# Another first pair of an attention and mixture-of-experts kernel: loads by head, first maxima with 64 rows, value work ahead of the exponentials

## The chip, the cores and the metric

The kernel runs on one core of a Trainium2 chip. The metric is the device time of one execution in microseconds (us), the median of several runs. One execution is recorded by the hardware profiler; its trace gives every row in this document. TensorE is PE, VectorE is DVE, ScalarE is ACT, GpSimd is POOL, and SyncE is SP, which only issues transfers.

## The reference: pooled-query attention, then a mixture of experts

Only the attention matters here. For 8 batches of 8 heads, 1152 positions and 64 dimensions each:

```python
q_pool = q.reshape(B, H, S // factor, factor, D).mean(axis=3)      # 576 queries
scores = scale * np.matmul(q_pool, k.transpose(0, 1, 3, 2))
scores = scores - np.max(scores, axis=-1, keepdims=True)
attn = np.exp(scores)
attn = attn / (np.sum(attn, axis=-1, keepdims=True) + 1e-09)
return np.matmul(attn, v).astype(np.float32)
```

The result (4608 tokens of 512) is routed to one of 8 experts, each of two matrix products.

## The kernel before

**Pairs.** The attention runs over 32 pairs. A pair is the same head of two batches: head one (of the pair) lies on partitions 0 to 63, head two on 64 to 127. `load_kq` and `load_v` bring keys `rawk` (128 x 1152), queries `rawq` (two halves of 576 columns, which are added for the pooling) and values `rawv`. Fetching runs ahead: while one pair's exponentials are made, the next pair is split and placed, and the one after is loaded.

**Exact products from 16-bit parts.** Keys and queries are split into a rounded part (`hi`, `qh`, by ACT) and a rest (`lo`, by POOL, seven subtractions). SP's queue then copies them into `B1` and `B2` of the pair (`place_q`, `place_k`, `place_lo`; tile `B` in the trace), from which each score is two matmuls (`scores`, lines 877 and 878). A row of `B2` holds the negative maximum of every query, in 16 bits (`mr`), so that the matmul subtracts it.

**Maxima.** A rough score from `hi` and the rounded queries `QB` gives the maxima. `QB` is block-diagonal: 9 blocks `u` of 128 queries, 0 to 3 and the lower half of 4 of head one, the rest of head two; what a head doesn't use is zero, cleared by DVE at the start. For pair 0, `first_max` multiplies blocks 0 to 4 with three thirds of the keys in 15 matmuls (`psc` and `pm` are banks of PSUM), and DVE reduces each (line 836); `row` then takes the maximum (`m`), has PE transpose it (line 783) and DVE round it (`mr`), and a transfer on ACT's queue writes it into `B2` (line 793). `maxpass` does blocks 5 to 8 of pair 0, and all of later pairs, between the scores (lines 812, 820).

**Exponentials and values.** A bank of 432 scores is exponentiated by ACT into `Pe` (line 879), four for each of six groups of a pair; the low half of the exponential's bits, `Pl`, is made by ACT (line 860) and DVE (line 862). The values get a common power of two as scale: ACT squares and sums them (`square`, line 720), PE sums over partitions (`power`), DVE makes the scale in five small operations (`scales`). `values` rounds them to `VH` (ACT, two parts) and makes the rest `vl` (POOL for pairs 0 and 1); `shifted` makes `VS`, a copy of `VH` times 2^-16. `pv` multiplies: three matmuls on `VH`, `vl` and `VS`.

**What sets the order.** The order on each engine is the order in which the program is written; an engine waits at an instruction until its inputs are there, with all behind it. Before the loop the first pair is written out by hand. In the loop each step writes some scores, maxima and value products, and tables give the step at which a pair's work is written. For pair 0, `V0` does so for the squares, the scale, `VH`, `VS` and `vl`; `LAG0` is the number of steps between a group of exponentials and its products with the values. The transfers share eight semaphores: each waits for the one eight earlier.

Of the kernel before, what the change touches and what calls it, by code (L numbers as in the profile page):

```python
# [574 lines left out]
def attention(tc, ctx, att, ident, npairs, xpool, on_two, on_split, on_scale, jobs, side, set_pm, started, ahead, hip):  # L575
# [35 lines left out]
    half_q = lambda i: slice(i * 288, (i + 1) * 288)  # L611

    def load_kq(p):
        k, q = (pa.tile([P, S], F32, name="raw" + x) for x in "kq")
        st[p]["k"], st[p]["q"] = k, q
        if p == 0:
            two = lambda x: x.rearrange("p (w n) -> p w n", w=2)
            for x, i in ((q, 0), (k, 0), (k, 1), (q, 1), (k, 2)):
                if x is q:
                    nc.sync.dma_start(out=two(q)[:, :, half_q(i)], in_=two(att[p, :, S:2 * S])[:, :, half_q(i)])  # L620
# [144 lines left out]
    def shifted(p):  # L765

        need(p, "vh0", "vh1")
        made.add((p, "vs"))
        o, v = (flat(x[p % 3])[:, :, 0:D] for x in (VS, VH))
        if p:  # L770
            nc.vector.tensor_single_scalar(o, v, 2.0 ** -16, op=ALU.mult)
        else:
            nc.scalar.activation(o, v, AF.Copy, scale=2.0 ** -16)
# [55 lines left out]
    def first_max(p):  # L829
# [3 lines left out]
        for i, (u, t) in enumerate([(u, t) for us in ((0, 1), (2, 3, 4)) for t in range(3) for u in us]):  # L833
            pt = ps_sc.tile([P, 512], F32, name="psc") if i % 2 else ps_max.tile([P, 512], F32, name="pm")
            nc.tensor.matmul(pt[:, 0:384], QB[p % 2][:, u], s["hi"][:, t * 384:(t + 1) * 384], start=True, stop=True)
            nc.vector.tensor_reduce(mp[:, u, t:t + 1], pt[:, 0:384], op=ALU.max, axis=AX.X)
# [170 lines left out]
    nc.scalar.activation(warm, warm, AF.Exp)
# [11 lines left out]
    for n, i in ((0, 0), (2, 1), (2, 2)):  # L1019
        if i < 2:  # L1020
            both = st[0]["q"].rearrange("p (w n) -> p w n", w=2)
            nc.vector.tensor_tensor(both[:, 0, half_q(i)], both[:, 0, half_q(i)], both[:, 1, half_q(i)], op=ALU.add)
        if i == 0:
            nc.scalar.copy(qb[0:D, half_q(0)], q0[0:D, half_q(0)])
        split_hi(0, i)
        if i == 1:
            nc.scalar.copy(qb[0:D, half_q(1)], q0[0:D, half_q(1)])
# [22 lines left out]
    drain(first)  # L1050
    mp0 = st[0]["mp"]
    for i in range(3):
        nc.gpsimd.memset(VH[i][:, :, :, D:D + 2], 1.0)
        nc.gpsimd.memset(VS[i][:, :, :, D:D + 2], 2.0 ** -16)
    for pe, pl in PT:
        for x in (slice(0, D), slice(D + W3, 2 * D + W3)):
            nc.gpsimd.memset(pe[:, x].bitcast(F32), 0.0)
            nc.gpsimd.memset(pl[:, x], 0.0)
    nc.gpsimd.memset(B2[1][D:D + 1, 0:2 * S], ROW)
# [472 lines left out]
```

## Time and profile before

| | us |
|---|---|
| median of 3 runs | 1150.68 (1149.37 to 1151.63) |
| the profiled execution | 1149.96 |
| its span | 1148.3 |
| busy: PE, DVE, ACT, POOL | 1105.8, 978.9, 914.7, 419.5 |
| first rough score on PE | 5.16 after the start |
| first exponential | 19.24 |
| first product with values | 31.05 |

A row of the timeline has its start and its duration in us, the engine, the line of the kernel, the operation with its output and input, and in brackets how long the engine had been idle and what ended that. A duration includes the latency of the result, so instructions of one engine can overlap. SPq and ACTq are issues of transfers; when the data land is not in the row.

### The profile page before, as it was taken

Reading aid. Unit: us, or ns where it says so; the run is one execution under the profiler, and the core shown is the slowest. Engines: PE = TensorE matmul, PEld = TensorE weight load, DVE = VectorE, ACT = ScalarE, POOL = GpSimd, SP = SyncE. Lnnn points to the kernel's source line nnn. Section 1 sums busy time; section 2 is a strip of 40 time slices with the busy share of each in tenths; the row PEclk is TensorE's granted clock in tenths of the full one; section 3 lists DMA queues with packets and bytes.
Section 4 is the critical chain, followed back from the end, with each engine's and each line's share of the span. In section 5 each row is a group of like instructions: output and inputs, shape, how many; then the busy total and the mean of one; then the engine's idle time right before and its main releaser. Section 6 shows DMA issues by size and latency. Waiting matters only on the chain. (4 is left out here: it accounts for less than half of the span.)

```text
span 1148.3 us, 36571 instructions
## 1 busy us (share of the span) xinstructions
PE 1105.8 (96%) x14963; PEld 813.4 (71%) x14963; DVE 978.9 (85%) x1961; ACT 914.7 (80%) x1463; POOL 419.5 (37%) x408
## 2 busy tenths in 40 slices
PE   5999999999999999999999989999999999999995
PEld 2777777777777777777777767866676676766763
DVE  6999999999999999999999999888976667576661
ACT  5999999999999999999999989766556666565561
POOL 6854444454453454434445331233222311211201
PEclk9999999999999999999999999999999999999998
DMA  7767858867758768669768463699989999989970
GB/s 226 195 174 177 192 156 175 191 162 181 190 149 203 172 165 199 156 170 193 171 167 185 129 132 77 222 279 283 283 243 267 316 274 295 278 268 285 252 250 22
DMA packets 175568, 232.65 MB, mean 203 GB/s; under 512 B 92351, under 2 KB 126799, under 8 KB 175392
## 3 DMA queue, kind: packets, MB, share of 16 engines
q1 hardware_dynamic: 169254, 210.45, 70.8%
q0 software_dynamic: 6128, 19.78, 6.4%
q8 instruction: 119, 1.95, 0.7%
q14 instruction: 57, 0.47, 0.2%
q10 hardware_dynamic: 10, 0.00, 0.0%
HBM read 146.11 MB, written 19.18 MB: 144 GB/s over the span
## 5 line engine op out<-in xcount | busy, mean ns | idle before, releaser
L879 ACT ACTIVATE Pe<-psc 128x432 int32<-128x432 f32 x768 | 377.7, 526 | 46.0 <-PE psc L878 36.0
L813 DVE TENSOR_REDUCE mp<-pm 128x1 f32<-128x512 f32 x566 | 373.3, 684 | 16.8 <-PE pm L812 8.9
L936 PE MATMUL xp<-VH,Pe 128*128 128x65 f16 x2880 | 372.6, 193 | 0.0
L938 PE MATMUL xp<-VS,Pl 128*128 128x65 f16 x2880 | 371.9, 193 | 0.4 <-DVE Pl L862 0.4
L937 PE MATMUL xp<-vl,Pe 128*128 128x64 f16 x2880 | 370.7, 192 | 0.0
L937 PEld LDWEIGHTS <-Pe 128*128 128x128 f16 x2880 | 267.6, 98 | 87.6
L878 PE MATMUL psc<-B 65*128 65x432 f16 (+2 forms) x1152 | 305.7, 288 | 2.2 <-DMA B<-mr 2.2
L877 PE MATMUL psc<-B 128*128 128x432 f16 (+2 forms) x1152 | 305.0, 287 | 1.7 <-ACT Pe L879 1.5
L936 PEld LDWEIGHTS <-Pe 128*128 128x128 f16 x2880 | 272.0, 98 | 45.7 <-issue 7.9
L938 PEld LDWEIGHTS <-Pl 128*128 128x128 f16 x2880 | 266.5, 97 | 0.6 <-DVE Pl L862 0.5
L860 ACT ACTIVATE Pl<-Pe 128x1152 f16<-128x1152 uint16 (+1 forms) x190 | 219.3, 1154 | 6.0
L812 PE MATMUL pm<-hi,QB 128*128 128x512 f16 x566 | 215.1, 382 | 8.4 <-DVE mp L813 8.1
L761 POOL TENSOR_SCALAR VH<-rawv,sc 128x512 f16<-128x512 f32 (+1 forms) x60 | 103.4, 1732 | 154.3 <-PE xp L938 73.7
L674 POOL TENSOR_TENSOR lo<-rawk,hi 128x576 f16<-128x576 f32 (+1 forms) x68 | 87.7, 1292 | 196.9 <-ACT hi L658 184.0
L1271 PE MATMUL ph<-xpart,w1h 128*128 128x256 f16 x544 | 148.3, 273 | 0.0
L1273 PE MATMUL ph<-xpart,w1l 128*128 128x256 f16 x544 | 148.3, 273 | 0.0
L1272 PE MATMUL ph<-xpart,w1h 128*128 128x256 f16 x544 | 148.3, 273 | 0.0
L878 PEld LDWEIGHTS <-B 65*128 65x128 f16 x1152 | 113.1, 98 | 26.8 <-issue 3.3
L877 PEld LDWEIGHTS <-B 128*128 128x128 f16 x1152 | 112.8, 98 | 9.7 <-issue 4.5
L1318 PE MATMUL po<-w2l,hh 128*128 128x512 f16 x296 | 112.2, 379 | 0.0
L1319 PE MATMUL po<-w2h,hl 128*128 128x512 f16 x296 | 112.2, 379 | 0.0
L1317 PE MATMUL po<-w2h,hh 128*128 128x512 f16 x296 | 112.2, 379 | 0.0
(260 smaller groups left out, 1775.9 us busy)
## 6 DMA issues: line engine op xcount, KB each, us to landing
w2r<-in_w_dram SPq DMA_DIRECT2D x76, 512.0 KB
w1r<-in_w_dram SPq DMA_DIRECT2D x72, 512.0 KB
rawv<-in_att_dram SPq DMA_DIRECT2D x32, 576.0 KB
B<-hi SPq DMA_DIRECT2D x128, 144.0 KB
rawq<-in_att_dram SPq DMA_DIRECT2D x31, 576.0 KB
rawk<-in_att_dram SPq DMA_DIRECT2D x31, 576.0 KB
B<-qh SPq DMA_DIRECT2D x128, 72.0 KB
B<-lo SPq DMA_DIRECT2D x64, 144.0 KB
```

Source lines behind the costliest of these rows:

```text
L812: nc.tensor.matmul(pm, QB[p % 2][:, u], s["hi"][:, t * 512:(t + 1) * 512], start=True, stop=True)
L813: nc.vector.tensor_reduce(mp[:, u, t:t + 1], pm, op=ALU.max, axis=AX.X)
L860: nc.scalar.activation(low, rest, AF.Copy, scale=LOW)
L877: nc.tensor.matmul(o, b1[:, ks], b1[:, qs], start=True, stop=False, skip_group_check=True)
L878: nc.tensor.matmul(o, b2[:, ks], b2[:, qs], start=False, stop=True, skip_group_check=True)
L879: nc.scalar.activation(Pe[:, D + x0:D + x1], pt, AF.Exp, scale=1.0 / 16)
L936: nc.tensor.matmul(out, Ph[:, qs], vh[:, c, j, 0:D + 1], start=c == 0 and g == 0, stop=False, skip_group_check=True)
L937: nc.tensor.matmul(out[:, 0:D], Ph[:, qs], vl[:, c, j], start=False, stop=False, skip_group_check=True)
L938: nc.tensor.matmul(out, Pl[:, qs], vs[:, c, j, 0:D + 1], start=False, stop=c == NKC - 1, skip_group_check=True)
L1271: nc.tensor.matmul(o, hi[:, c, fs], xh[:, :, c], start=c == 0, stop=False)
L1272: nc.tensor.matmul(o, hi[:, c, fs], xl[:, :, c], start=False, stop=False)
L1273: nc.tensor.matmul(o, lo[:, c, fs], xh[:, :, c], start=False, stop=c == 3)
```

## The change

It touches the first pair alone, with what stands beside it in the queues.

- **Loads.** The queries of head one come in two halves on ACT's queue, ahead of ACT's table load; its keys in three thirds on SP's; then head two's queries and keys, one transfer each. Before, each part had both heads.
- **First maxima.** The blocks 0 to 3 use 64 rows (head one) of `QB` and `hi`, block 4 all 128. Both adds of head one's query halves stand ahead of the first reduce on DVE; head two's add is put among the reduces, and its rounding on ACT behind the three thirds of head one.
- **Values.** Squares, scale, `VH` and `vl` of pair 0 are written ahead of the loop, hence ahead of the exponentials (`V0` is gone). `VS` of pair 0 goes from ACT to DVE.
- **POOL.** It clears the second `B2`, the edges of `VH`, `VS`, `Pe` and `Pl` first; the subtractions of pair 0 follow, then the first step of pair 1, `vl`, and the subtractions of pair 1 (before: pair 1's subtractions, then the clears).
- **Pair 1.** The rounding of its queries (`split_qh`) and its subtractions are written at the end of step 0, behind two exponentials.
- `LAG0` goes from 7 to 5: products with the values stand two steps earlier.

In the listings of order below, `x2` behind a row stands for two equal rows, numbers behind a name tell buffers apart, and `QB_112` is pair 0's, `QB_114` pair 1's. ACT from its first instruction, before:

```order
L1007 ACT_TABLE_LOAD
L1007 ACTIVATE warm<-warm 128x1
L1024 CAST QB_112<-rawq 64x288
L658 CAST hi<-rawk 128x384 x2
L1027 CAST QB_112<-rawq 64x288
L658 CAST hi<-rawk 128x384
L1030 CAST qh<-rawq 128x576
L1031 CAST QB_112<-rawq 64x576
```

and after:

```order
L620 DMA rawq<-in_att_dram 64x2x288 x2
L1006 ACT_TABLE_LOAD
L1006 ACTIVATE warm<-warm 128x1
L1030 CAST hi<-rawk 64x384
L1032 CAST QB_112<-rawq 64x288
L1030 CAST hi<-rawk 64x384
L1032 CAST QB_112<-rawq 64x288
L1030 CAST hi<-rawk 64x384
L1038 CAST hi<-rawk 64x1152
```

The two issues are ahead of the table, and each cast of keys or queries has 64 rows. ACT from the row of maxima on, before:

```order
L793 DMA B_0_111<-mr 1x5x128
L879 ACTIVATE Pe_115<-psc 128x432 x2
L720 ACTIVATE vl,ss<-rawv 128x1152
L879 ACTIVATE Pe_115<-psc 128x432
L860 ACTIVATE Pl_116<-Pe_115 128x1152
L879 ACTIVATE Pe_115<-psc 128x432
L763 ACTIVATE VH_123<-rawv,sc 128x10x64
L879 ACTIVATE Pe_117<-psc 128x432 x2
L763 ACTIVATE VH_123<-rawv,sc 128x8x64
L773 ACTIVATE VS_124<-VH_123 128x18x64
```

and after:

```order
L720 ACTIVATE vl,ss<-rawv 128x1152
L790 DMA B_0_111<-mr 1x5x128
L660 CAST hi<-rawk 128x384 x2
L763 ACTIVATE VH_123<-rawv,sc 128x10x64
L763 ACTIVATE VH_123<-rawv,sc 128x8x64
L660 CAST hi<-rawk 128x384
L877 ACTIVATE Pe_115<-psc 128x432 x2
L650 CAST qh<-rawq 128x576
L877 ACTIVATE Pe_115<-psc 128x432
```

The squares are ahead of the row's transfer, both `VH` and three roundings of pair 1's keys between it and the first exponential, and `VS` is gone. DVE behind the maxima's blocks 5 to 8 of pair 0, before:

```order
L813 TENSOR_REDUCE mp<-pm 128x1 x8
L821 TENSOR_REDUCE mp<-pm 128x4
L779 TENSOR_REDUCE m_330<-mp 128x4
L732 TENSOR_SCALAR half<-pm 128x1
L734 TENSOR_SCALAR sc<-half 128x1 x2
L734 TENSOR_SCALAR scales<-half 128x1
L734 TENSOR_SCALAR both<-half 64x1
L792 TENSOR_SCALAR mr<-pj 4x128
```

and after:

```order
L810 TENSOR_REDUCE mp<-pm 128x1 x8
L770 TENSOR_SCALAR VS_124<-VH_123 128x18x64
L818 TENSOR_REDUCE mp<-pm 128x4
L776 TENSOR_REDUCE m_352<-mp 128x4
L789 TENSOR_SCALAR mr<-pj 4x128
L860 TENSOR_SCALAR Pl_116<-Pe_115 128x576
```

`VS` stands between the eight reduces and the last one (of four blocks), from which `m`, the transposition on PE and the row `mr` follow. SP behind pair 0's placing, before:

```order
L609 DMA B_187<-hi 64x1152 x2
L609 DMA QB_114<-qh 64x576 x2
L624 DMA rawq<-in_att_dram 128x1152
L625 DMA rawk<-in_att_dram 128x1152
L629 DMA rawv<-in_att_dram 128x1152
L793 DMA B_0_111<-mr 1x4x128
```

and after:

```order
L608 DMA B_220<-hi 64x1152 x2
L626 DMA rawq<-in_att_dram 128x1152
L627 DMA rawk<-in_att_dram 128x1152
L608 DMA QB_114<-qh 64x576 x2
L631 DMA rawv<-in_att_dram 128x1152
L790 DMA B_0_111<-mr 1x4x128
```

The queries of pair 1 for its rough scores (`QB_114`) are copied behind pair 2's loads of queries and keys, no longer ahead of them.

The core of the diff:

```diff
-V0 = (0, 1, (2, 3), 3, (3, 4))
-LAG0 = 7
+LAG0 = 5
...
         if p == 0:
-            for x, i in ((q, 0), (k, 0), (k, 1), (q, 1), (k, 2)):
-                if x is q:
-                    nc.sync.dma_start(out=two(q)[:, :, half_q(i)], in_=two(att[p, :, S:2 * S])[:, :, half_q(i)])
-                else:
-                    nc.sync.dma_start(out=k[:, i * 384:(i + 1) * 384], in_=att[p, :, i * 384:(i + 1) * 384])
+            for i in range(2):
+                nc.scalar.dma_start(out=two(q[half[0]])[:, :, half_q(i)], in_=two(att[p, half[0], S:2 * S])[:, :, half_q(i)])
+            for i in range(3):
+                nc.sync.dma_start(out=k[half[0], third(i)], in_=att[p, half[0], third(i)])
+            nc.sync.dma_start(out=q[half[1]], in_=att[p, half[1], S:2 * S])
+            nc.sync.dma_start(out=k[half[1]], in_=att[p, half[1], 0:S])
...
-        if p:
-            nc.vector.tensor_single_scalar(o, v, 2.0 ** -16, op=ALU.mult)
-        else:
-            nc.scalar.activation(o, v, AF.Copy, scale=2.0 ** -16)
+        nc.vector.tensor_single_scalar(o, v, 2.0 ** -16, op=ALU.mult)
...
-            nc.tensor.matmul(pt[:, 0:384], QB[p % 2][:, u], s["hi"][:, t * 384:(t + 1) * 384], start=True, stop=True)
+            r = slice(0, P if u == 4 else D)
+            nc.tensor.matmul(pt[:, 0:384], QB[p % 2][r, u], s["hi"][r, third(t)], start=True, stop=True)
...
+    load_kq(0)
     nc.scalar.activation(warm, warm, AF.Exp)
     nc.gpsimd.memset(ones, 1.0)
-    load_kq(0)
     load_v(0)
     for i in range(2):
         nc.vector.memset(QB[i], 0.0)
-    nc.gpsimd.memset(B2[0][D:D + 1, 0:2 * S], ROW)
+    for i in range(2):
+        nc.gpsimd.memset(B2[i][D:D + 1, 0:2 * S], ROW)
+    for i in range(3):
+        nc.gpsimd.memset(VH[i][:, :, :, D:D + 2], 1.0)
+        nc.gpsimd.memset(VS[i][:, :, :, D:D + 2], 2.0 ** -16)
+    for pe, pl in PT:
+        for x in (slice(0, D), slice(D + W3, 2 * D + W3)):
+            nc.gpsimd.memset(pe[:, x].bitcast(F32), 0.0)
+            nc.gpsimd.memset(pl[:, x], 0.0)
...
+    for i in range(2):
+        nc.vector.tensor_tensor(q0[half[0], half_q(i)], q0[half[0], half_q(i)], q1[half[0], half_q(i)], op=ALU.add)
+    for i in range(3):
+        nc.scalar.copy(hi[half[0], third(i)], k0[half[0], third(i)])
+        if i < 2:
+            nc.scalar.copy(qb[half[0], half_q(i)], q0[half[0], half_q(i)])
+        for _ in range(2):
+            next(first)
+    next(first)
+    nc.vector.tensor_tensor(q0[half[1]], q0[half[1]], q1[half[1]], op=ALU.add)
+    nc.scalar.copy(hi[half[1]], k0[half[1]])
+    nc.scalar.copy(qb[half[1], SQ:S], q0[half[1]])
     nc.scalar.copy(st[0]["qh"], q0)
+    square(0)
...
+    drain(first)
+    power(0)
+    ends(0)
+    st[0]["row"]()
     if npairs > 1:
         split_q(1)
-        for i in range(3):
+        for i in range(2):
             split_hi(1, i)
-        split_qh(1)
-        for i in (3, 4, 5, 6, 0, 1, 2):
-            split_lo(1, i)
+    values(0, 0, False)
+    values(0, 1, False)
+    values(0, 0, True)
+    values(0, 1, True)
+    if npairs > 1:
+        split_hi(1, 2)
+        at(0, 0, lambda: split_qh(1))
+        at(0, 0, lambda: [split_lo(1, i) for i in (3, 4, 5, 6, 0, 1, 2)])
+    at(0, 0, lambda: shifted(0))
```

More of the change, by code (lines that the diff above doesn't have):

```diff
@@ L611, in attention @@
     half_q = lambda i: slice(i * 288, (i + 1) * 288)
+    third = lambda i: slice(i * 384, (i + 1) * 384)
+    half = [slice(0, D), slice(D, P)]
     def load_kq(p):
@@ L687, in place @@
         place_k(p, (0, 1))
-    half = [slice(0, D), slice(D, P)]
     def place_q(p, heads):
@@ L832, in first_max @@
         mp = s["mp"] = sm.tile([P, 9, 3], F32, name="mp")
-        for i, (u, t) in enumerate([(u, t) for us in ((0, 1), (2, 3, 4)) for t in range(3) for u in us]):
+        for i, (u, t) in enumerate([(u, t) for us in ((0, 1), (2, 3), (4,)) for t in range(3) for u in us]):
             pt = ps_sc.tile([P, 512], F32, name="psc") if i % 2 else ps_max.tile([P, 512], F32, name="pm")
-            nc.tensor.matmul(pt[:, 0:384], QB[p % 2][:, u], s["hi"][:, t * 384:(t + 1) * 384], start=True, stop=True)
+            r = slice(0, P if u == 4 else D)
+            nc.tensor.matmul(pt[:, 0:384], QB[p % 2][r, u], s["hi"][r, third(t)], start=True, stop=True)
             nc.vector.tensor_reduce(mp[:, u, t:t + 1], pt[:, 0:384], op=ALU.max, axis=AX.X)
             yield
-        row(p, mp, 0, 5)()
+        s["row"] = row(p, mp, 0, 5)
     def scores(p, j, r):
@@ L1012, in attention @@
         nc.vector.memset(QB[i], 0.0)
-    nc.gpsimd.memset(B2[0][D:D + 1, 0:2 * S], ROW)
+    for i in range(2):
[7 more added lines that the diff above has]
+            nc.gpsimd.memset(pl[:, x], 0.0)
     split_q(0)
-    q0, qb = st[0]["q"][:, 0:SQ], QB[0].rearrange("p u n -> p (u n)")
+    qb = QB[0].rearrange("p u n -> p (u n)")
+    q0, q1 = (st[0]["q"][:, i * SQ:(i + 1) * SQ] for i in range(2))
+    k0, hi = st[0]["k"], st[0]["hi"]
     if npairs > 1:
@@ L1018, in attention @@
     first = first_max(0)
-    for n, i in ((0, 0), (2, 1), (2, 2)):
+    for i in range(2):
+        nc.vector.tensor_tensor(q0[half[0], half_q(i)], q0[half[0], half_q(i)], q1[half[0], half_q(i)], op=ALU.add)
+    for i in range(3):
+        nc.scalar.copy(hi[half[0], third(i)], k0[half[0], third(i)])
         if i < 2:
[L1021 to L1027, printed above, removed]
+            nc.scalar.copy(qb[half[0], half_q(i)], q0[half[0], half_q(i)])
         for _ in range(2):
             next(first)
+        made.add((0, f"hi{i}"))
+    next(first)
+    nc.vector.tensor_tensor(q0[half[1]], q0[half[1]], q1[half[1]], op=ALU.add)
+    nc.scalar.copy(hi[half[1]], k0[half[1]])
+    nc.scalar.copy(qb[half[1], SQ:S], q0[half[1]])
     nc.scalar.copy(st[0]["qh"], q0)
-    nc.scalar.copy(qb[D:P, SQ:S], q0[D:P])
+    square(0)
     for i in (3, 4, 5, 6, 0, 1, 2):
@@ L1042, in attention @@
     place_k(0, (1,))
+    drain(first)
+    mp0 = st[0]["mp"]
+    power(0)
+    ends(0)
+    st[0]["row"]()
     if npairs > 1:
         split_q(1)
-        for i in range(3):
+        for i in range(2):
             split_hi(1, i)
-        split_qh(1)
-        for i in (3, 4, 5, 6, 0, 1, 2):
-            split_lo(1, i)
[L1050 to L1059, printed above, removed]
+    values(0, 0, False)
[7 more added lines that the diff above has]
+    at(0, 0, lambda: shifted(0))
     mxq.append(maxpass(0, mp0))
@@ L1082, in attention @@
             go(T_LV, load_v)
-        sq, power_, vh, vs, vl = (T_SQ, T_POW, T_VH, T_VS, T_VL) if p > 1 else V1 if p else V0
+        if not p:
+            continue
+        sq, power_, vh, vs, vl = (T_SQ, T_POW, T_VH, T_VS, T_VL) if p > 1 else V1
         if p == 1:
```

## The prediction

> **What bounds the kernel now.** I read the totals of the engines first, then busy time by stretches, then the rows of the first 60 us engine by engine, because the change only moves work that is issued before the first pair's exponentials or shortly behind them.
>
> ```profile
> PE 1105.8 (96%) x14963; PEld 813.4 (71%) x14963; DVE 978.9 (85%) x1961; ACT 914.7 (80%) x1463; POOL 419.5 (37%) x408
> ...
> 0.00:25.00 25.00, 13.89 (x51) 6.00 (x52) 17.06 (x38) 11.62 (x21) 16.60 (x47) 1.00 0.80 248
> 25.00:50.00 25.00, 23.18 (x332) 16.26 (x330) 22.99 (x53) 24.70 (x43) 20.20 (x15) 1.00 0.64 167
> 75.00:100.00 25.00, 25.00 (x430) 19.23 (x426) 24.16 (x55) 23.59 (x41) 12.66 (x10) 1.00 0.86 195
> ```
>
> In a row of stretches (the last three) stand the stretch, then the busy time of PE, PEld, DVE, ACT and POOL, the granted clock (1.00) and the DMA. TensorE (PE) is busy 96% of the span and all of 75 to 100 us. Its work is the same in both kernels but for its order, so the change is worth as much as PE reaches a given place of its program earlier. Of the first 25 us PE loses 11.1, of the next 25 another 1.8. This is where to look:
>
> ```profile
> 15.02 0.37 PE L783 MATMUL pj<-ident,m 128*5 128x128 f32 x1 [2.38 <-DVE m L779]
> 18.69 0.52 PE L878 MATMUL psc<-B 65*128 65x432 f16 x1 [1.14 <-DMA B<-mr]
> 23.77 0.37 PE L783 MATMUL pj<-ident,m 128*4 128x128 f32 x1 [0.24 <-DVE half L732]
> 25.72 0.34 PE L877 MATMUL psc<-B 128*128 128x432 f16 x1 [0.46 <-ACT Pe L879]
> 27.25 0.38 PE L812 MATMUL pm<-hi,QB 128*128 128x512 f16 x1 [0.35 <-DVE mp L813]
> 31.05 0.19 PE L936 MATMUL xp<-VH,Pe 128*128 128x65 f16 x1
> ```
>
> So there are three stages: first maxima (to 15.02), the wait for the row of maxima (to 18.69), and a stage in which ScalarE (ACT) is late with the exponentials (to 31.05, the first product with the values). The chain through the second and third:
>
> ```profile
> 5.68 0.56 DVE L836 TENSOR_REDUCE mp<-pm 128x1 f32<-128x384 f32 x1 [1.45 <-PE pm L835]
> 9.46 0.56 DVE L836 TENSOR_REDUCE mp<-pm 128x1 f32<-128x384 f32 x1 [0.51 <-PE pm L835]
> 14.12 0.55 DVE L836 TENSOR_REDUCE mp<-pm 128x1 f32<-128x384 f32 x1
> 14.70 0.17 DVE L779 TENSOR_REDUCE m<-mp 128x5 f32<-128x15 f32 x1
> 15.43 0.28 DVE L792 TENSOR_SCALAR mr<-pj 5x128 f16<-5x128 f32 x1 [0.56 <-PE pj L783]
> 15.74 1.54 ACTq L793 DMA_DIRECT2D B<-mr  x1
> 19.24 0.53 ACT L879 ACTIVATE Pe<-psc 128x432 int32<-128x432 f32 x1 [4.60 <-PE psc L878]
> ```
>
> **A, first maxima.** From 9.46 to 14.12 stand ten steps of one reduce: 0.466 us each. Fifteen need 7.0 us; from 5.68 to 14.70 they take 9.0, since thirds of the keys and the second add come late. The change loads only head one's rows first, so fifteen should run without a break. When do they start?
>
> ```profile
> 0.81 0.47 SPq L620 DMA_DIRECT2D rawq<-in_att_dram  x1
> 0.81 1.28 ACT L1007 ACT_TABLE_LOAD   x1 [0.81 <-PEq L1519]
> 2.10 0.20 ACT L1007 ACTIVATE warm<-warm 128x1 f32<-128x1 f32 x1
> 4.61 0.51 ACT L658 CAST hi<-rawk 128x384 f16<-128x384 f32 x1
> 3.77 0.46 DVE L1022 TENSOR_TENSOR rawq<-rawq 128x288 f32<-128x288 f32 x1 [1.63 <-DMA rawq<-in_att_dram]
> 7.13 0.88 DVE L1022 TENSOR_TENSOR rawq<-rawq 128x288 f32<-128x288 f32 x1 [0.43 <-DMA rawq<-in_att_dram]
> 6.97 0.73 POOL L674 TENSOR_TENSOR lo<-rawk,hi 128x288 f16<-128x288 f32 x1 [1.05 <-ACT hi L658]
> 17.56 0.14 POOL L1053 MEMSET VH<- 128x36 f16 x1
> 19.45 2.01 POOL L1059 MEMSET B<- 1x2304 f16 x1
> 11.86 1.40 POOL L639 TENSOR_TENSOR rawq<-rawq 128x576 f32<-128x576 f32 x1
> ```
>
> ACT now issues two loads ahead of its table. An issue took 0.47 on SP and 1.54 on ACT (the maxima, beside SP's own issues); these two stand beside SP's three, and I take 0.95, twice a lone one: 0.81 + 1.9 + 1.28 + 0.2 = 4.2. Then two casts, of the keys and of the queries (0.51 in the row, 0.9 together since they overlap), and a matmul (0.48): the first reduce at 5.6, as before (5.68). Bounds: 4.6 with 0.47, 6.8 with 1.54. Data: 288 KB were there for the first add at 3.77 and 960 KB for the second at 7.13, so 200 KB a us; now the first add needs 144 KB (and 96 of keys beside it), the second 480, there at 4.7, and VectorE is free for the first reduce at 5.1. Behind the start: 15 x 0.466 = 7.0, and one add of 64x576 put among the reduces, twice the columns of the 0.46 row: 0.75 (up to 1.1 if it is held, as the one at 7.13 was beside GpSimd's subtraction). So m comes at 13.4 against 14.70. Squares and scale now stand on the chain too: the square follows five casts and three more of head two on ACT, starts near 10 and is done at about 11.5, where the maxima end at 13.3; the five small scale operations (0.15 the one at 23.63 below, some 0.1 each to the next) lie in the 0.56 that VectorE waits for the transposition. **A = -1.3**, bounds -2.3 to -0.1.
>
> A row speaks against it: the first add could be held by GpSimd, which now clears the second B from 3.5 to 5.5 (2.01 us). Held to its end, the first reduce moves to 6.9, A to 0 and the time to 1150.3. The row at 7.13 shows such a hold behind an operation that reads SBUF; no row shows one behind a clear. [...]
>
> **B, the row of maxima and the scores.** Issue and landing took 18.69 - 15.74 = 2.95 us; I leave them, so the scores start at 17.4. SP's copies of the low parts must be there: GpSimd first clears for 3.9 us more (1.9 the short ones, from 17.56 to 19.45, and 2.01 the second B), so behind the 3.5 us that it works at the start anyway it begins to subtract at 7.4, but without pauses: four of 0.73 and three of two thirds of it are 4.4 us and end at 11.8. They ended at 11.86 before, where the row of the next step begins. ACT behind that issue (14.4 + 1.54) still rounds pair 1's keys in three thirds (0.4 each without their overlap) and the values (rows below), 2.6 us, and gives the first exponential at 18.5 (19.24 before). What is late next is VectorE: the values' shifted copy moves to it, ahead of the last maximum of pair 0, whose row PE must transpose before its fifth bank.
>
> ```profile
> 23.63 0.15 DVE L732 TENSOR_SCALAR half<-pm 128x1 int32<-128x1 int32 x1
> 46.73 1.37 DVE L771 TENSOR_SCALAR VS<-VH 128x1152 f16<-128x1152 f16 x1
> 55.31 0.54 DVE L771 TENSOR_SCALAR VS<-VH 128x1152 f16<-128x1152 f16 x1
> 46.59 1.20 POOL L757 TENSOR_TENSOR vl<-rawv,VH 128x512 f16<-128x512 f32 x1
> 25.42 1.91 POOL L756 TENSOR_SCALAR rawv<-rawv,sc 128x640 f32<-128x640 f32 x1 [3.96 <-issue]
> ```
>
> It took 0.54 alone and 1.37 beside GpSimd's work on the values. Now it comes at about 21.2, and GpSimd's four steps on the values (1.91 the first, 1.20 the last, from 17 on) are running: I take 1.3. Of these 1.3 the 0.24 that PE waited there already is no loss. **B = +1.0**, bounds 0 and +1.4.
>
> **C, the late exponentials.** ACT loses the following work behind the first exponential:
>
> ```profile
> 20.82 1.16 ACT L720 ACTIVATE vl<-rawv 128x1152 f16<-128x1152 f32 x1
> 24.43 0.82 ACT L763 ACTIVATE VH<-rawv,sc 128x640 f16<-128x640 f32 x1
> 25.97 0.73 ACT L763 ACTIVATE VH<-rawv,sc 128x512 f16<-128x512 f32 x1
> 26.73 1.16 ACT L773 ACTIVATE VS<-VH 128x1152 f16<-128x1152 f16 x1
> 13.98 0.67 ACT L648 CAST qh<-rawq 128x576 f16<-128x576 f32 x1
> ```
>
> 1.2 + 0.7 + 0.6 + 1.1 = 3.6 us go, pair 1's rounding of queries (0.6) comes in. But from 30 us on PE is full anyway, so no more is to be had than PE loses. From 25.3 to 31.05 it issues four banks of scores (0.37 each, 25.72 to 26.09), nine matmuls for maxima (0.21 each, three in 0.81 with the last one's end) and four short ones, about 3.6 us in 5.8: 2.2 are lost. With LAG0 at 5 the first products with values stand behind the eighth bank, not the eleventh, and fill gaps; waits for VectorE's maxima (0.35 at 27.25) stay, 0.8 in all. **C = -1.4**, bounds -2.0 and -0.8.
>
> **Sum**: -1.3 + 1.0 - 1.4 = -1.7. The profiled execution took 1149.96 (span 1148.3), so 1148.3; the median of the runs shown is 0.7 above that execution, so I forecast 1149.0 against 1150.68. Everything else that moves is covered: GpSimd's clears by the load of head two, pair 1's low parts (now 23 to 28 us) by the first pair's 24 exponentials, behind which pair 1's scores stand.
>
> **Rivals.**
> Fast: the shifted copy isn't held (B = 0): -2.7, 1148.0; with short ACT issues too (A = -2.3): -3.7, 1147.0. I take 1147.5. For it: 0.54 at 55.31, 0.47 at 0.81. Against: GpSimd works on the values just then.
>
> [...]
>
> Slower: the queries of pair 1 come late to PE.
>
> ```profile
> 16.62 1.18 SPq L609 DMA_DIRECT2D QB<-qh  x2
> 26.09 0.81 PE L812 MATMUL pm<-hi,QB 128*128 128x512 f16 x3
> GB/s 0 26 324 231 224 354 378 422 414 365 220 192 134 126 191 201 163 152 393 418 422 160 1 66 130 112 109 225 234 235 201 272 306 330 232 332 232 124 7 3
> ```
>
> QB<-qh was issued at 16.62 and used at 26.09, and stood ahead of pair 2's loads. Now ACT rounds these queries behind two exponentials (19.5 to 20.1), SP issues until 21.4, behind loads of 1.15 MB. In the last row (slices of 1.125 us) such loads ran at 400 from 20.2 on; 1.15 MB are 2.9 us. I expect it at 23.5, used at 24.9. Every us past 24.9 stops PE, with the scores queued behind it; past 26.6 the gain is gone. With 8 us from issue to landing (29.4) the kernel would take 1153.5.
>
> **Numbers.** Forecast case 0.50 (1148.2 to 1150.2), fast 0.27, half loads or a held add 0.15, slower 0.08. The range, 1146.6 to 1151.3, leaves out the slower case and the end of the fast one. 0.2% (2.3 us) is about what a measurement of this kernel can tell from no change: the fast case and 0.15 of the forecast's lie below 1148.4, so 0.42 faster, 0.50 the same, 0.08 slower.
>
> **What would show it.** A: first reduce near 5.6, m near 13.4, reduces 0.47 apart. B: maxima landed near 17.4, the VS row at 1.3 and PE waiting for m of 4 rows. C: no wait for Pe between 24 and 30, the first xp near 26. I am wrong if PE waits for QB, for B<-lo, or if the first cast of ACT starts past 5.5.

## The result, and the profile after

The changed kernel is slower by a little: 1152.82 us (1148.79 to 1155.82, 22 runs) against 1150.74 (1148.48 to 1153.32, 22 runs of the kernel before), a ratio of 1.002 [1.0012, 1.0027]. The forecast was 1149.0. The profiled execution took 1152.26 (span 1150.6) and stands 0.6 below the median, that of before (1149.96) 0.8 below its own, so the two traces may be compared as they are. Totals and stretches of the profile after:

```profile
PE 1105.2 (96%) x14963; PEld 813.0 (71%) x14963; DVE 980.5 (85%) x1963; ACT 915.9 (80%) x1463; POOL 419.9 (36%) x408
...
25.00:50.00 25.00, 22.96 (x334) 16.37 (x335) 22.41 (x46) 21.32 (x36) 17.75 (x17) 0.94 0.66 175
75.00:100.00 25.00, 24.29 (x421) 18.66 (x418) 23.33 (x53) 23.06 (x40) 11.89 (x9) 1.00 0.96 198
```

The work of every engine is as long as before to within 2 us. PE however isn't full where the prediction had it full: 24.29 of the stretch from 75 to 100 us against 25.00 before. In its timeline (start, duration, what; in brackets the idle time before and what ended it) the first three rows answer to the three stages shown of before, and the others are new stops:

```profile
14.48 0.37 PE L780 MATMUL pj<-ident,m 128*5 128x128 f32 x1 [1.42 <-DVE half L732]
17.36 0.52 PE L876 MATMUL psc<-B 65*128 65x432 f16 x1 [0.34 <-DMA B<-mr]
26.40 0.26 PE L934 MATMUL xp<-VH,Pe 128*128 128x65 f16 x1
...
22.82 0.27 PE L780 MATMUL pj<-ident,m 128*4 128x128 f32 x1 [2.52 <-DVE m L776]
25.15 1.46 PE L809 MATMUL pm<-hi,QB 128*128 128x512 f16 x3 [0.54 <-DMA QB<-qh]
42.01 0.39 PE L809 MATMUL pm<-hi,QB 128*128 128x512 f16 x1 [0.94 <-DMA QB<-qh]
92.61 0.34 PE L876 MATMUL psc<-B 65*128 65x432 f16 x1 [0.71 <-DMA B<-mr]
137.43 0.34 PE L876 MATMUL psc<-B 65*128 65x432 f16 x1 [0.73 <-DMA B<-mr]
226.02 0.34 PE L876 MATMUL psc<-B 65*128 65x432 f16 x1 [0.51 <-DMA B<-mr]
```

The three stages end 0.5, 1.3 and 4.7 us earlier than before, as meant. Then PE stops at 42.01 for pair 2's queries (`QB<-qh`), and at 92.61, 137.43 and 226.02 for rows of maxima (`B<-mr`) of pairs 3, 5 and 9.

To see where time goes I followed single VectorE instructions through the traces: the start of the same instruction in a kernel, less its start in the first profiled execution of before. For the kernel after this is +1.2 us at 58, 0.0 at 77, +0.9 at 95, +1.6 at 143, +2.1 at 227, +1.5 at 768 and +2.1 at 1131 (times of before). The start of pair 1's maxima, by contrast, was ahead by 0.7:

```profile
25.79 2.48 DVE L810 TENSOR_REDUCE mp<-pm 128x1 f32<-128x512 f32 x4 [2.02 <-PE pm L809]
```

Before (VectorE's timeline of before):

```profile
26.50 4.88 DVE L813 TENSOR_REDUCE mp<-pm 128x1 f32<-128x512 f32 x8 [1.48 <-PE pm L812]
```

So the lead of 0.7 at 26 us has become a lag of 1.2 at 58. By 77 the two are level again (before itself stops in between, 0.55 us at 69.91 for pair 2's row of maxima), and 2 us more go between 77 and 227, far behind the change. Why is pair 2's `QB` late? Pair 1's low parts on GpSimd and some of the issues on SP, first before:

```profile
13.32 2.79 POOL L674 TENSOR_TENSOR lo<-rawk,hi 128x288 f16<-128x288 f32 x4
16.07 1.56 POOL L674 TENSOR_TENSOR lo<-rawq,qh 128x192 f16<-128x192 f32 x3
...
27.79 2.46 SPq L609 DMA_DIRECT2D B<-lo  x4
33.73 1.34 SPq L625 DMA_DIRECT2D rawk<-in_att_dram  x1
35.17 1.15 SPq L609 DMA_DIRECT2D QB<-qh  x2
86.60 0.80 SPq L793 DMA_DIRECT2D B<-mr  x1
```

and after:

```profile
24.72 2.79 POOL L676 TENSOR_TENSOR lo<-rawk,hi 128x288 f16<-128x288 f32 x4
27.47 1.56 POOL L676 TENSOR_TENSOR lo<-rawq,qh 128x192 f16<-128x192 f32 x3
...
29.06 2.83 SPq L608 DMA_DIRECT2D B<-lo  x4
31.93 2.52 SPq L608 DMA_DIRECT2D B<-hi  x4
34.50 0.58 SPq L626 DMA_DIRECT2D rawq<-in_att_dram  x1
35.12 0.44 SPq L627 DMA_DIRECT2D rawk<-in_att_dram  x1
35.67 1.41 SPq L608 DMA_DIRECT2D QB<-qh  x2
86.61 0.80 SPq L790 DMA_DIRECT2D B<-mr  x1
```

The low parts are done at 29.0 instead of 17.6. SP's first copy of them waits for them (from 26.68 on, where the copies ahead of it are issued), and behind it in SP's queue stand the copies of pair 1's rounded keys, two loads of pair 3, and pair 2's `QB`. The `QB` copies are issued only 0.5 later than before. But pair 3's loads ahead of them, 576 KB each, are issued 1.6 and 1.4 later, and by the trace's semaphore events the second of these landed at 41.59 instead of 40.48. Right behind it landed the first copy of `QB`, for which PE waits, at 41.96 instead of 40.80, and the second at 42.42 instead of 41.04. Pair 3's row was issued at the same time in both (86.6) and landed at 92.56 instead of 90.99.

### The profile page after: what moved, and what is told of

It is laid out like the page before. It is cut to its first block, busy times and chain, and to the rows that moved or that the text cites. A ratio compares the mean times of both kernels' runs of the same rounds, so it can differ in the third digit from the quotient of the medians.

```text
span 1150.6 us, 36571 instructions
## 1 busy us (share of the span) xinstructions
PE 1105.2 (96%) x14963; PEld 813.0 (71%) x14963; DVE 980.5 (85%) x1963; ACT 915.9 (80%) x1463; POOL 419.9 (36%) x408
## 5 line engine op out<-in xcount | busy, mean ns | idle before, releaser
L810 DVE TENSOR_REDUCE mp<-pm 128x1 f32<-128x512 f32 x566 | 373.1, 684 | 17.4 <-PE pm L809 10.0
L1290 DVE SCALAR_TENSOR_TENSOR hl<-ph,hh 128x512 f16<-128x512 f32 x72 | 49.7, 690 | 73.9 <-ACT hh L1289 73.2
```

The source lines that it names most:

```text
L810: nc.vector.tensor_reduce(mp[:, u, t:t + 1], pm, op=ALU.max, axis=AX.X)
```

## The experiments

Six theories are spoken of. **1, hand-over:** pair 1's late low parts make all later SP issues late, and so PE waits for pair 2's and 3's queries. **2:** `VS` on VectorE makes PE idle for 2.5 us, and a half clock for 3.4 us follows. **3:** the new first transfers slow later ones. **4:** VectorE is full from 26 us on, so only the start of pair 1's maxima counts. **5:** rows of maxima of odd pairs land 4 to 6 us after their issue, behind a transposing transfer in the same queue, and PE stops where it is over about 5. **6:** before stands at a lucky spot, and executions differ by 1 to 3 us of themselves. All ratios are to before on the same chip. A trace is one execution: those of `a_alone` and `after_turn` ran 3.1 and 3.7 us under the medians of their kernels, that of `b_lag5` 3.7 over, the others within 2.

**Parts of the change.** `a_alone` is before with only the loads, first adds and first maxima of the change. The other three are edits of after: a longer lag, pair 1's splitting ahead of the values as before the change, and `VS` three steps later.

```diff
-LAG0 = 5                                       # lag7
+LAG0 = 7
...
+        split_hi(1, 2); split_qh(1)            # p1_early: ahead of values(0, 0, False)
+        for i in (3, 4, 5, 6, 0, 1, 2):
+            split_lo(1, i)
...
-    at(0, 0, lambda: shifted(0))               # vs3
+    at(3, 0, lambda: shifted(0))
```

> The kernel before with part A alone: loads by head in finer parts (two on ACT's queue), both adds first, first maxima with 64 rows. Values, GpSimd's order, pair 1's split and LAG0 stay as before. Theory 1 (hand-over: the lead of some 2 us is won, and lost between 41 and 72 us because pair 1's low parts and all that SP issues behind them come later): A's lead of about 1.3 us stays, since pair 1's split is not moved: 1149.4 where before is 1150.7. Theory 2 (VS holds the last maximum, PE idles 2.5 us and its clock halves for 3.4 us): no VS on VectorE here, also 1149.4. Theory 3 (the new first transfers themselves, half the partitions and two more issues, make later transfers land late, the rows of maxima above all): as slow as the change, about 1152.8, with the rows of maxima again landing 6 us after their issue near 92 and 137 us. Theory 4 (VectorE is full from 26 us on, so only the start of pair 1's maxima counts): that start moves by about 1 us, the end by no more than 0.7: 1150.0 to 1150.7.

> The changed kernel with LAG0 at 7 again. Theories 1, 2 and 3: as the change within 0.8 us (1152 to 1153.6), since the products with the values do not set the hand-over, the hold or the transfers; PE shows more idle time near 28 us and correspondingly less at 42 and 50 us. Rival: the earlier products are what puts PE ahead of the prefetch and then out of step; then about 1150.7.

> The changed kernel with the rounding of pair 1's queries, the last third of its keys and its seven subtractions written ahead of the values again, as in the kernel before. Theory 1: SP's copies of pair 1's low parts are issued near 25 instead of 29.06, pair 2's queries some 1 to 2 us earlier than 35.67, PE does not wait for them at 42, and the end comes 1.5 to 2.5 us earlier than the change: 1150.3 to 1151.3. Against it stands that the rest of the values (vl) then comes 4.4 us later, near 28, and the first products wait for it. Theories 2 and 3: as the change, 1152 to 1153.6.

> The changed kernel with VS of pair 0 written at step 3, behind the last maximum and its row mr on VectorE, no longer ahead of them. All theories: PE's wait of 2.52 at 22.82 falls to about 1.2. Theory 2: the clock stays full, and the end comes 1 to 2 us earlier than the change: 1150.8 to 1151.8. Theories 1, 3 and 4: the earlier start is lost again by 72 us (pair 2's queries land at 42 all the same): 1152 to 1153.6.

Measured: `a_alone` 1.0021 [1.0006, 1.0036], `lag7` 1.0031 [1.002, 1.0042], `p1_early` 1.0056 [1.0038, 1.0074], `vs3` 1.0029 [1.0013, 1.0044]. None is faster than before. PE in `vs3`:

```profile
22.27 0.27 PE L780 MATMUL pj<-ident,m 128*4 128x128 f32 x1 [0.62 <-DVE m L776]
25.54 0.82 PE L809 MATMUL pm<-hi,QB 128*128 128x512 f16 x3 [1.40 <-DMA QB<-qh]
42.46 0.39 PE L809 MATMUL pm<-hi,QB 128*128 128x512 f16 x1 [1.59 <-DMA QB<-qh]
```

The wait behind `VS` is gone (2.52 to 0.62), pair 1's queries stop PE instead, and the time doesn't move: theory 2 falls as the cause. In `p1_early` the low parts were done at 21.4 and pair 2's `QB` was issued 1.9 earlier than in after (33.79), as theory 1 wants. Pair 1's maxima began at 24.63, 1.9 before those of before, so theory 4, by which that start alone counts, doesn't carry the result either. But PE, early itself, stopped for 1.29 until 40.83, where the first copy of `QB` had landed, and then:

```profile
55.93 0.21 POOL L179 CAST wg<-wg 128x32 bf16<-128x32 f32 x1 [3.51 <-DMA wg<-in_w_gate_dram]
66.80 0.39 PE L809 MATMUL pm<-hi,QB 128*128 128x512 f16 x1 [2.71 <-DMA QB<-qh]
```

GpSimd waited 3.51 us for the router's weights (a small load that the program places at a step of its own), with pair 3's subtractions behind it, and pair 3's `QB` came 2.7 us late. `a_alone` shows the same, smaller (GpSimd's 1.40 for `wg`, PE's 1.39 at 65.11). In both this load stands behind pair 2's copies in SP's queue and was issued at 52.11 and 51.33; in before it stands ahead of them and was issued at 40.68. So here a lead is lost at a transfer that didn't move with it. The 1150.3 to 1151.3 that theory 1 forecast for `p1_early` did not come: its median is 1156.21. `lag7` had a wait of 2.98 for pair 2's `QB` at 44.34; its time is no different from after's.

**Later constants, and the transposition behind the row.** SP's queue also carries the transposition of an earlier group's result (`xt`), issued shortly ahead of an odd pair's row. In before: `83.55 1.43 SPq L920 DMA_TRANSPOSE`, then the row at 86.60. One edit puts it behind the row, the other moves the router's constants nine steps on.

```diff
-            turn_part(p, 0, xh)                # b_turn, after_turn: out of split_x
+        turn_part(p, 0, xh)                    # into turned, behind the row
...
-T_RT = 24                                      # b_rt33, a_alone_rt33
+T_RT = 33
```

> The kernel before with both transposing transfers of every second pair (xt<-x) issued behind the row of maxima mr on SP's queue; before and after have the first of the two ahead of it. Theory 5 (the rows of maxima of every second pair land 4 to 6 us after their issue because a transposing transfer is in flight ahead of them; PE stops where that is over some 5.1 us): these rows land within 2.5 us, PE never waits for one behind 72 us, the time falls by 0.5 to 1.5 (before loses little there in its trace, 0.49 at 578) and its spread narrows. Rival: the rows are late for the other transfers in flight (loads, copies of queries); landing stays at 4 to 6 us and the time as before.

> The changed kernel with the same edit. Its trace lost 0.88, 0.73, 0.65 and 0.37 at rows of maxima that landed late (92, 137, 226 and 316 us), 2.6 in all, and stood level with before at 72 us. Theory 5: these losses go, the time is 1149.7 to 1150.5, level with the kernel before with the same edit within 0.7. Theory 3 (the new first transfers themselves slow the later ones) : still 1.5 to 2.5 us over that kernel.

> The kernel before with the small loads of the router (wg, bias, idt) and GpSimd's constants for it at step 33 instead of 24, that is behind pair 3's rounded queries on GpSimd, where it is idle for 7 us. It is the control for the next kernel: PE did not wait for QB before, so no change within 0.8 us (1149.0 to 1151.0).

> Part A alone (as run earlier) with the same move to step 33. There PE waited 1.39 us at 65.11 for QB of pair 3, whose rounding on GpSimd (61.97) stood behind these constants, and those behind the small loads (waits of 1.40 for wg and 1.64 for idt). Theory 1 (a lead is lost at the hand-over to the next pairs' queries): the wait goes, the lead of 0.8 us at 57 us is still there at 75 us, and the time is 0.8 to 1.3 below before. Theory 3: no gain, 1152 to 1153, and the rows of maxima land later than in the kernel before with the same move.

Measured: `b_turn` 1.0024 [1.0008, 1.004], `after_turn` 1.0035 [1.0022, 1.0047], `b_rt33` 1.0012 [1.0, 1.0023], `a_alone_rt33` 1.003 [1.0014, 1.0045]. In `after_turn` the rows of pairs 3 to 9 landed 2.1 to 4.2 us after their issue and PE no longer stopped for them: its lag from 77 to 227 us is -0.3 to -0.6, not +0.0 to +2.1. That much of theory 5 is shown. The time that it forecast (1149.7 to 1150.5) did not come: the median is 1154.38, and the trace is the fastest of its 12 executions. In their traces both kernels lost 2 to 3 us from 709 to 768 us, where ACT waits for the first expert's weights. ACT in before, then in `b_turn`, and PE behind it in `b_turn`:

```profile
725.79 1.06 ACT L1473 ACTIVATE w1h<-rawk 128x1024 f16<-128x1024 f32 x1 [0.86 <-DMA rawk<-in_w_dram]
```

```profile
725.38 1.06 ACT L1473 ACTIVATE w1h<-rawk 128x1024 f16<-128x1024 f32 x1 [2.19 <-DMA rawk<-in_w_dram]
...
726.91 0.28 PE L877 MATMUL psc<-B 128*128 128x288 f16 x1 [2.00 <-ACT Pe L879]
```

With the later constants the waits for `QB` at 65 us are gone, but the lead, 1.9 us at 77 in `a_alone_rt33`, went at the row of pair 3:

```profile
91.61 0.34 PE L880 MATMUL psc<-B 65*128 65x432 f16 x1 [1.62 <-DMA B<-mr]
```

`b_rt33` lost 2.25 at the same place (93.15).

**Copies, and the rest of the change alone.** `b_copy` and `after_copy` are the two kernels unchanged, `b_lag5` is before with `LAG0 = 5`, and `no_a` is after with the loads and first maxima of before.

> The kernel before, unchanged, a second time: its runs against those of the kernel before give what two equal kernels differ by, and its trace shows what changes from one execution to the next. All theories: ratio 1.000 within 0.0008. New theory 6 (the kernel before stands at a lucky spot: the landing of the rows of maxima and the steps behind the attention vary by 1 to 3 us from one execution to the next): the trace again stands within 0.3 us of the first one up to 250 us, and differs later by the landing of single rows.

> The changed kernel, unchanged, a second time. If the losses at the rows of maxima near 92, 137 and 226 us belong to the change, they are there again in this trace within 0.3 us each and the ratio is 1.0015 to 1.0025. If they are chance, they stand at other rows or are gone in this trace, though the ratio may be the same.

> The kernel before with LAG0 at 5: part C of the forecast alone, without loads, values or pair 1's split moved (the values come as late as before, so the first products wait for VH and VS on PE). By the forecast's own working some of the 2.2 us that PE loses from 25 to 31 us would be had: up to -0.8. Theory 4 (VectorE is full from 26 us on, and pair 2's queries land when they land): no gain, 0 to +1.

> The changed kernel with the loads and first maxima of the kernel before (part A undone; values ahead of the exponentials, VS on VectorE, GpSimd's order and LAG0 as changed). Theory 3 (the new first transfers slow the later ones): back to before, 1150 to 1151. Theory 1 (pair 1's late low parts and what follows on SP's queue): as slow as the change or slower, 1152 to 1154.5, since the start of the scores is 1.3 us later and the hand-over no earlier.

Measured: 1.0003 [0.9994, 1.0012], 1.0033 [1.0022, 1.0044], 1.0005 [0.999, 1.0019] and 1.0016 [1.0006, 1.0025]. So the difference of before and after is real, and it comes without the new transfers as well (theory 3 isn't needed for it). `LAG0` alone brings nothing: with 5 the products with values come before GpSimd's `vl` of the kernel before.

```profile
27.85 0.19 PE L937 MATMUL xp<-vl,Pe 128*128 128x64 f16 x1 [1.90 <-POOL vl L757]
```

In `no_a` the low parts are again done at 29.04, and pair 2's `QB` landed at 42.39 and 42.70:

```profile
42.44 0.39 PE L808 MATMUL pm<-hi,QB 128*128 128x512 f16 x1 [2.08 <-DMA QB<-qh]
```

Of the stops of after two stand in its copy, smaller: 0.37 at 92.70 and 0.54 at 137.33. Those at 226 us and, for pair 2's `QB`, at 42 us are not there. The clock differs between the two. The same matmul of 432 columns (and that of the maxima, of 512), first in after, then in `after_copy`, whose last row is the place at which after stopped at 42.01:

```profile
19.77 0.35 PE L875 MATMUL psc<-B 128*128 128x432 f16 x1
27.17 0.55 PE L875 MATMUL psc<-B 128*128 128x432 f16 x1
```

```profile
25.36 0.57 PE L875 MATMUL psc<-B 128*128 128x432 f16 x1
29.01 0.62 PE L809 MATMUL pm<-hi,QB 128*128 128x512 f16 x1
31.70 0.38 PE L809 MATMUL pm<-hi,QB 128*128 128x512 f16 x1
42.31 0.38 PE L809 MATMUL pm<-hi,QB 128*128 128x512 f16 x1
```

After is at full speed at 19.77, for some 3.4 us at half speed around 27 (by the trace's clock records from 24.74 to 28.15), and then full again; its copy is at half speed until past 29 (0.62 for 512 columns) and full from 31.70 (0.38). Working at half speed, PE comes to pair 1's maxima at 26.08 in the copy (25.15 in after), and VectorE stands 1.1 behind before at 33 us, where after is 0.5 ahead. So PE reaches the place of pair 2's `QB` at 42.31, when its first copy has been there since 41.92, and doesn't wait. `after_again`, run later, does the same (42.22 and 42.02). In the two copies the lead was thus gone before the hand-over could take it; at 77 us the three stand at 0.0, +0.4 and +0.3. `vs3` had the full clock from 21.05 on and waited 1.59 for `QB`, so the half clock isn't needed for the loss. That it costs nothing isn't shown.

**The rows on another queue.** Rows of odd pairs to ACT's queue, in three kernels; and `a_mid`, after with two of pair 1's seven subtractions ahead of `vl` again.

```diff
-            done = (nc.sync if p or u0 else nc.scalar).dma_start(
+            done = (nc.sync if (p or u0) and p not in (3, 5, 7, 9, 11) else nc.scalar).dma_start(
...
+        split_lo(1, 3); split_lo(1, 4)         # a_mid: ahead of values(0, 0, True)
```

> The changed kernel with the rows of maxima of pairs 3, 5, 7, 9 and 11 issued on ACT's queue instead of SP's, where they stand behind loads, a store and a transposing transfer in flight. Theory 5 (these rows are late because SP's transfers land in the order of issue): they land within 2.5 us, PE does not wait for them at 92, 137 and 226 us, the trace stands within 0.8 us of before at 250 us (it was 2.1 and 1.5 behind), and the time is 1.0 to 1.6 below the change: 1151.3 to 1152. It costs ACT five issues of 0.8 to 1.3 us. Rival (all DMA work is shared, the queue doesn't matter): landing stays at 4 to 6 us, the time as the change.

> The kernel before with the same edit, the control. Its two traces lost 0 and 0.4 at these rows, so no gain: 1149.7 to 1151.

> Part A alone, the router's constants at step 33, and these rows on ACT's queue. Its trace without the last edit was 2.0 us ahead of before at 91 us and lost 1.8 at pair 3's row. If the lead of the start is lost only at the hand-over and these rows, it stays: 1148.5 to 1149.3, faster than both kernels. If a lead is lost in any case (VectorE and PE full, other late transfers behind 300 us), 1150 to 1151.5.

> The changed kernel with two of pair 1's seven subtractions ahead of the values' rest on GpSimd (which waited 2.4 us there for VH). Theory 1: pair 1's low parts are done at 27.6 instead of 29.1, pair 2's queries issued and landed 1.0 to 1.5 us earlier (41.2 instead of 42.5 to 43), VectorE's scale of pair 2 at 49 instead of 49.9, and the time 0.5 to 1.2 below the change. Rival (the hand-over costs nothing that is not lost behind 72 us anyway): as the change within 0.4.

Measured: 1.0063 [1.0047, 1.0079], 1.0031 [1.002, 1.0041], 1.0044 [1.0032, 1.0057] and 1.0014 [1.0005, 1.0022]. Another queue didn't free the row. From ACT in `after_mract`, and what PE then did:

```profile
88.76 0.78 ACTq L790 DMA_DIRECT2D B<-mr  x1
...
43.91 0.39 PE L809 MATMUL pm<-hi,QB 128*128 128x512 f16 x1 [2.89 <-DMA QB<-qh]
181.05 0.28 PE L875 MATMUL psc<-B 128*128 128x288 f16 x1 [0.48 <-ACT Pe L877]
```

The row landed at 93.91, 5.1 us after its issue, between the landings of the two transpositions (92.65 and 94.28), and its issue now costs ACT, so that PE waits for exponentials. The 1151.3 to 1152 that theory 5 forecast became 1156.53. The test isn't clean: with the row gone from SP, SP issued a second transposition ahead of it (88.20). The 5.1 us lie within the 4.3 to 6.3 that the rows of pairs 3 to 9 took on SP's queue in before and after. So no run shows that SP's queue makes the row late, and of theory 5 stays what was measured: with a transposition in flight the row of pair 3 was late on either queue (5.96 us in after, 5.1 here).

`a_mid` is the first edit of after that comes nearer to before, though on another chip and with overlapping intervals (1.0014 against 1.002 to 1.0033). Its low parts were done at 28.2 instead of 29.0, and `QB` stopped PE less:

```profile
41.49 0.39 PE L809 MATMUL pm<-hi,QB 128*128 128x512 f16 x1 [0.17 <-DMA QB<-qh]
```

**More of the same, beside after.** `a_hi` takes the third rounding of pair 1's keys and four subtractions to the place ahead of pair 0's row; three subtractions and the queries' rounding stay late. `after_again` is after, unchanged.

```diff
+        for i in (3, 4, 5, 6):                 # a_hi: ahead of st[0]["row"]()
+            split_lo(1, i)
...
-        at(0, 0, lambda: [split_lo(1, i) for i in (3, 4, 5, 6, 0, 1, 2)])
+        at(0, 0, lambda: [split_lo(1, i) for i in (0, 1, 2)])
```

> The changed kernel with the rounding of pair 1's keys (three casts) ahead of the row's transfer on ACT, where ACT waited, and all four subtractions of pair 1's keys ahead of the values' rest on GpSimd, where it waited for VH; the three of its queries stay behind. Theory 1 (pair 1's low parts, 11 us later than before on GpSimd, and SP's queue behind them cost the 2 us): they are done near 26.5 (29.1 in the change, 28.1 in a_mid), pair 2's queries land near 41 (42.4 to 43.1), VectorE's scale of pair 2 comes near 48.5 (49.7 to 50.1), pair 3's row of maxima lands before 91, and the time is 1.5 to 2.5 us below the change on the same chip, level with before within 1 us. Rival (later landings and the experts' first weights decide by themselves): as the change within 0.8 us.

> The changed kernel, unchanged, beside a_hi on the same chip: ratio to before 1.0020 to 1.0033 as in the two calls so far; its trace again behind before by about 0.9 us at 95 us and 1.4 to 1.6 at 143 us.

Measured: `a_hi` 1.0012 [1.0, 1.0024], 1151.58; `after_again` 1.0023 [1.0011, 1.0036], 1153.01; before 1150.59. GpSimd and SP in `a_hi`:

```profile
15.89 2.79 POOL L676 TENSOR_TENSOR lo<-rawk,hi 128x288 f16<-128x288 f32 x4
25.09 1.56 POOL L676 TENSOR_TENSOR lo<-rawq,qh 128x192 f16<-128x192 f32 x3
...
27.15 2.46 SPq L608 DMA_DIRECT2D B<-lo  x4
34.92 1.11 SPq L608 DMA_DIRECT2D QB<-qh  x2
```

`QB` landed at 40.56 and 40.80 (42.02 and 42.69 in `after_again`), and PE waited for it in neither. Where the traces stand against the first trace of before:

| us of before | 58 | 95 | 143 | 227 | 709 | 768 | 1131 |
|---|---|---|---|---|---|---|---|
| `b_copy` | +0.1 | -0.5 | -0.1 | -0.1 | -0.3 | -0.8 | 0.0 |
| after | +1.2 | +0.9 | +1.6 | +2.1 | +1.9 | +1.5 | +2.1 |
| `after_copy` | +0.7 | +1.0 | +1.5 | +1.6 | +1.0 | +1.6 | +1.3 |
| `after_again` | +0.6 | +0.3 | +0.6 | +1.2 | +0.7 | +3.2 | +3.3 |
| `a_mid` | -0.2 | -0.5 | -0.7 | -0.8 | +0.1 | +1.6 | +1.8 |
| `a_hi` | 0.0 | -0.6 | -0.5 | +0.3 | +0.9 | +2.0 | +2.4 |
| `p1_early` | -0.3 | +2.4 | +2.9 | +3.6 | +3.5 | +6.5 | +4.6 |
| `a_alone` | -0.8 | 0.0 | +0.4 | +0.3 | -0.2 | -1.2 | -0.6 |
| `no_a` | +2.3 | +1.1 | +1.0 | +0.8 | +1.3 | +1.8 | +2.2 |
| `b_lag5` | +1.8 | +0.8 | +1.0 | +2.1 | +2.2 | +4.3 | +4.7 |

With part of the subtractions early (`a_mid`, `a_hi`) the kernel stands level with before at 58 us and 0.5 to 0.7 ahead past the rows at 95 and 143. With all of them late (after and both copies) it is 0.6 to 1.2 behind at 58, and more time is lost at the rows. At the end only `a_alone` is ahead, in its fast execution. By medians no version beat before.

The step from 709 to 768 us has two parts. In `after_again`, `b_turn` and `b_lag5` PE waits 1.7 to 2.0 us behind the expert's weights, and then its clock is at half for 3.41 us. The same matmul of 432 columns in `after_again`, in that stretch and behind it:

```profile
730.34 0.55 PE L875 MATMUL psc<-B 128*128 128x432 f16 x1
734.73 0.34 PE L875 MATMUL psc<-B 128*128 128x432 f16 x1
```

In `after_again` the lag goes from +0.7 to +1.7 with the wait and to +3.1 with the half clock, in `b_turn` from -1.8 to -0.4 and +1.0. These 1.4 us stay to the end. So the half clock does set the time at this place, where PE is full.

## Why the prediction was wrong

**A, forecast -1.3: oversized, and for the most part not where it was put.** VectorE at the start, after (second add, first and eighth reduce, head two's add, maximum):

```profile
5.79 0.45 DVE L1028 TENSOR_TENSOR rawq<-rawq 64x288 f32<-64x288 f32 x1 [1.15 <-DMA rawq<-in_att_dram]
6.17 0.54 DVE L834 TENSOR_REDUCE mp<-pm 128x1 f32<-128x384 f32 x1
...
9.53 0.76 DVE L1037 TENSOR_TENSOR rawq<-rawq 64x576 f32<-64x576 f32 x1
10.31 0.56 DVE L834 TENSOR_REDUCE mp<-psc 128x1 f32<-128x384 f32 x1
...
14.16 0.17 DVE L776 TENSOR_REDUCE m<-mp 128x5 f32<-128x15 f32 x1
```

ACT's two issues took 1.51 together (1.9 forecast) and its first cast came at 3.76. But the second half of the queries was there only at 5.79, not at 4.7, and all reduces stand behind that add: the first at 6.17 for 5.6. The reduces are 0.47 apart, with the add of 0.76 (0.75 forecast) among them, and `m` is there at 14.16 for 13.4. That is -0.5 against before's 14.70, inside the bounds. The row landed at 17.22 for 17.4, 1.4 before that of before; but in six executions that share before's start it landed at 17.4 to 18.64 (mean 17.9), and the one that I forecast from is the latest of them. Against the mean the gain is some 0.7, and it came between the maximum and the landing: `m` started at 14.04 to 14.70 in the same six (mean 14.36) and at 14.08 to 14.45 in the ten kernels with the changed start of after (mean 14.28), so the maxima themselves gained about 0.1. Half loads and a held add share a chance of 0.15. No run shows a half rate for loads on 64 rows: head one's queries and two thirds of its keys, 480 KB, had landed at 5.77, where the 200 KB a us of before gave 4.7. The held add isn't there (0.45 each beside GpSimd's clears).

**B, forecast +1.0: the mechanism as told, but not a bound.** `VS` took 1.35 at 20.61 beside GpSimd's work, as I took it (1.3 at 21.2), and PE waited 2.52 for the maximum behind it. `vs3` took the wait away and the time stayed. So B wasn't a term of the end: behind it the next input, pair 1's queries, was late as well (1.40 at 25.54 in `vs3`).

**C, forecast -1.4: what it names happened, and nothing came of it.** PE waited for no `Pe` between 24 and 30 us, and the first product came at 26.40 (forecast 26). Yet `b_lag5` stands at 1.0005 and `lag7` isn't told apart from after. The lost 2.2 us on PE were filled, in part by matmuls at half clock (24.74 to 28.15), and pair 1's maxima began only 0.7 earlier.

**The step that failed** is the sentence behind the sum: pair 1's low parts "by the first pair's 24 exponentials, behind which pair 1's scores stand", together with "from 30 us on PE is full anyway". The cover was reckoned for one user, pair 1's scores, and they were indeed not late. The other users are the instructions behind the waiting one in SP's queue: its copies of the low parts waited until 29.06, and behind them stood pair 1's rounded keys, pair 3's loads and pair 2's `QB`, which PE needs at 41. Its price at 42.01 was 0.94 in after, 1.59 in `vs3` and 2.08 in `no_a`; 0.17 in `a_mid` and nothing in `a_hi`, where part of the low parts is done early. It was nothing either in the two copies of after and in `after_turn`, where the clock was at half until 29.5, 26.5 and 30.1 us and PE came later than `QB`. That the hand-over takes the lead away is therefore shown in the trace of after, with `a_hi` beside it, which has its half clock at nearly the same time (25.3 to 28.7): from 39 to 50 us after goes from -0.3 to +1.3, `a_hi` from +0.3 to +0.2. On the clock it is supported rather than shown: by medians `a_hi` is 1.4 below `after_again` on the same chip, but the two intervals overlap.

The second half of the loss stands where the prediction didn't look. The rows of pairs 3, 5, 7 and 9 took 4.3 to 6.3 us to land in before and after, and PE stopped at most of those that took over 5.5 and at a few that took less: 0.71, 0.73 and 0.51 in after (landings of 5.96, 6.25 and 5.34), 0.32 and 0.61 at the later two places in `after_again`. `after_turn` shows that a transposition ahead of the row has a part in it, since without it the rows landed in 2.1 to 4.2 us and the stops are gone. Before has the same transposition ahead of its rows, and why they land later in after isn't shown: pair 3's row took 5.96 and 5.62 us in after and `after_copy`, but 4.29 in `after_again`, as in before (4.39).

The rival for a slower kernel, pair 1's queries, was real (0.54 at 25.15, the condition at 24.9 named) but small. It was the right kind, one pair too early: the copies in the same queue for the next pair.

**What stays open.** Before's lead at 709 to 768 us is explained only in part: ACT's wait for the first expert's weights is 0.86 there, 1.73 in `a_mid` and 2.19 in `b_turn`, and why it differs is open, as is why the half clock follows it in three executions and not in `after_turn`, where PE waited longest (2.42). `a_alone` has a median 2.8 above before's though its trace is 0.6 below, so a single trace can't tell of 2 us (its 12 runs lie between 1149.41 and 1155.64). That before stands at a lucky spot of its queues (theory 6) is argued from fifteen variants that are all a little slower or the same, not shown.

## What to carry to other kernels

When work is put off because its first user is late anyway, follow the queue that carries its result: in after, SP's queue stood from 26.68 to 29.06 us at the first copy of pair 1's low parts, and everything behind it was put off too, also for the pairs after. Two kernels are compared at a place where each has done the same work: with `LAG0` at 5 VectorE's order near 57 us is another than with 7, so the lags here start at 58. A start that is earlier by 1 us is worth something only if all the transfers on the way to the end move with it; here loads, copies and rows of maxima were placed by step, and each held the lead in one trace or another. Before a gain of 0.1% is forecast from a single trace, its starting point should be looked up in several executions, since one late landing there can be most of it.

## What the runs showed of the hardware

In before and after a row of maxima of 2.2 KB landed 1.8 to 2.4 us after its issue in pairs 4, 6, 8 and 10, and 4.3 to 6.3 in pairs 3, 5, 7 and 9, where a transposing transfer was in flight. With these rows on ACT's queue (`after_mract`, `b_mract`, `a_rt33_mract`) it was 4.3 to 7.0. In pair 11 one was in flight at the issue as well, and the row landed after 1.84 in before and in after.

Equal programs got the full clock at different times: by the clock records at 17.9, 29.5 and 19.7 us in three executions of after, and in the first and third it fell to half again for 3.41 us (from 24.7 and from 23.1 on). At 77 us the three stand within 0.4 us of each other. At 728 to 735 us, where PE is full, such a half clock of 3.41 us cost 1.4 us in each of three executions.
